# Batch 0's raw f32 products with 128 columns of phi instead of 64, and the expert probabilities loaded after the first key and value blocks

## The chip, the cores and the metric

The kernel runs on one core of one Trainium2 chip. The metric is the device time of one execution in microseconds (us). The engines are named as in the profile: PE (TensorE matmul) with PEld (its weight loads), DVE (VectorE), ACT (ScalarE), POOL (GpSimd) and SP (SyncE, which issues the DMAs).

## The reference

Eight batches, eight heads, 576 rows, head size 64, 32 memory slots. Attention goes over a compressed memory, and its output feeds a mixture of four experts.

```python
a = softmax(phi)                              # (8, 8, 576, 32), over the 32 slots
k_m = einsum('bhsm,bhsd->bhmd', a, k)         # 32 compressed keys for each head
v_m = einsum('bhsm,bhsd->bhmd', a, v)
attn = softmax(q @ k_m.T / sqrt(64))
x = (attn @ v_m), heads side by side          # (4608, 512)
p = domain_probs / (domain_probs.sum(-1) + 1e-9)
out = sum over e of p[:, e] * (relu(x @ w1[e]) @ w2[e])      # 512 -> 1024 -> 512
```

## The kernel before

**The long part.** The batches are worked in four pairs. For each pair and each expert the kernel folds the compressed values into w1 (tile `vw`), so that a step is: `first_mm` (L518 to L520, softmaxed scores `AT` times `vw`), a relu on ACT and a residual on DVE, and `second` (L562 to L564, times `w2`). Each f32 operand is split into a high and a low part, three products in place of one. These steps fill nearly all of the time. The end of a step group scales by `p` from tile `pt`, which `probabilities()` has normalized.

**The start.** Until the first step can run, batch 0 must be prepared. This is the place of the change:

- `load_phi(0)` and then the loads of `pt` and of six tiles (`stage`: the raw keys and values `kv` of four head pairs, their last 64 rows `kvt`, and a block of q, `qm`) are issued on SP's queue, which runs in order.
- `keep_warm(10)` issues ten products of the identity with itself on PE (`warm`, L1747) while the loads are under way.
- phi's softmax is done in the transposed layout and turned by PE (`tpa`, `tpb`) into the tile `af`.
- `direct_mm(hp, w, ...)` multiplies, in plain f32, the raw keys (w = 0) or values (w = 1) of head pair hp as the stationary operand by 64 columns of `af` (32 slots for each of the two heads) as the moving one: four products of 128 rows (L278) and one with the tail of 64 rows (L279), summed in PSUM tile `xd`. In the profile each such f32 product is two matmul records, each with its weight load of 128 columns. There are eight calls, four head pairs by two. I call them groups 1 to 8 in the order in which they run.
- Of the product of two heads' values with two heads' slots only the diagonal blocks are wanted. `direct_pick` copies them from `xd` to `kvT`.
- `scores_mm` (L408, `sc`) multiplies q by the compressed keys, `direct_vw` (L292, `pv`) the compressed values by raw w1. On DVE `scores_max`, `scores_sub`, `soft_sum` and `soft_mul` (L418, L426, L437, L444) with an exponential on ACT make the softmax, and PE turns it (`tp`, L457) into `AT`.

**What sets the order.** `start_plan` lists these pieces as tasks with a cost, dependencies and due times, simulates the engines with them, and emits the code in the order of the simulated starts. Loads that are under way at the start have assumed landing times in `LANDED`; a task whose `lands` is set isn't started in the plan before that time. Each engine runs its own instructions in the order in which they were emitted.

A load whose buffer is still in use waits on SP's queue until that buffer is released (`free_key`), and the loads behind it wait too. The raw key and value tiles are released by the second product that reads them, in groups 5 to 8.

Of the kernel before, what the change touches and what calls it, by code (L numbers as in the profile page):

```python
# [9 lines left out]
F32 = mybir.dt.float32  # L10
# [6 lines left out]
B, H, S, D, M = 8, 8, 576, 64, 32  # L17
N, DM, E, F = 4608, 512, 4, 1024
P = 128
# [32 lines left out]
START_SIDE = 1400  # L52
START_LOOK = 150
GHOST = 4
LANDED = (7900, 8600, 9900, 11200, 12500, 13800, 16500, 17800, 19100, 15200)
START_AT = 27500
LEAD = 2000
HOLD = 2500
# [10 lines left out]
def body(ctx: ExitStack, tc: tile.TileContext, qm, qt, qh, kv, kvt, phi, phn, prob, w1, w2, res):  # L69
    nc = tc.nc  # L70
    pool = lambda name, **k: ctx.enter_context(tc.tile_pool(name=name, bufs=1, **k))
    const, wp, work, att = pool("const"), pool("wp"), pool("work"), pool("att")
    psum = pool("psum", space=PSUM)
# [3 lines left out]
    kvT = [const.tile([P, 2, NP, 2 * M], F32, name=f"kvT{i}") for i in range(2)]  # L77
    for t in kvT:
        nc.gpsimd.memset(t, 0.0)
    pt = const.tile([P, N // P, E], F32, name="pt")  # L80
# [31 lines left out]
    def stage_ahead(upto):  # L112
        while count[0] < min(upto, len(order)):
            i, src = count[0], source(order[count[0]])
            tag, bufs = ring(i)
            t = work.tile([P, 1024], F32, name="stage", tag=tag, bufs=bufs)
            n = 1
            for d in src.shape[1:]:
                n *= d
            names = "abcd"[:len(src.shape) - 1]  # L120
            t = t[:src.shape[0], :n].rearrange(
                f"p ({' '.join(names)}) -> p {' '.join(names)}", **dict(zip(names, src.shape[1:]))
            )
            nc.sync.dma_start(t, src)
            staged[i] = t
            count[0] += 1
# [13 lines left out]
    def take_key(key):  # L140
        assert order[count[1]] == key and count[1] in staged, (key, count)
        raws[key] = staged.pop(count[1])
        count[1] += 1

    def free_key(key):
        del raws[key]
        released.add(numbers[key])
        stage_released()
# [21 lines left out]
    def w1_hi(raw, fh, hp):  # L170
        t = w1t[fh, hp] = new_w1()
        nc.scalar.copy(t[:, 0, :], raw[:, hp % 2, :])
# [5 lines left out]
    def w2_hi(j):  # L178
        t = w2t[0, 0, j] = wp.tile([P, 2, DM], F32R, name="w2", tag="w2", bufs=NJ)
        nc.scalar.copy(t[:, 0, :], raws["w2", 0, j // 2][:, j % 2, :])  # L180
# [6 lines left out]
    st = {}  # L187

    def load_phi(b):
        ph = att.tile([P, 2, 640], F32, name="ph", tag="ph")  # L190
        for g in range(2):
            nc.sync.dma_start(ph[:, g, :S], phi[b, g])
        st["ph", b] = ph

    def phi_max(b, g):
        nm = att.tile([P, 1], F32, name="nm", tag="nm", bufs=2)
        nc.vector.reduce_max(nm, st["ph", b][:, g, :S], AX.X)
        nc.vector.tensor_scalar_mul(nm, nm, -1.0)
        st["nm", b, g] = nm

    def phi_exp(b, g):
        ph = st["ph", b][:, g, :S]
        zs = att.tile([P, 1], F32, name="zs", tag="zs", bufs=2)
        nc.scalar.activation(ph, ph, AF.Exp, bias=st["nm", b, g], accum_out=zs)
        st["zs", b, g] = zs

    def phi_norm(b, g, tail=True):
        ph, zs = st["ph", b][:, g], st["zs", b, g]
        nc.vector.tensor_scalar_add(zs, zs, 1e-9)
        nc.vector.reciprocal(zs, zs)  # L210
        nc.vector.tensor_scalar_mul(ph[:, :S], ph[:, :S], zs)
        if tail:
            nc.vector.tensor_copy(ph[:, S:], ph[:, 512:S])
# [58 lines left out]
    def direct_mm(hp, w, raw, tail):  # L272

        if hp % 2 == 0:
            st["xd", w, hp // 2] = psum.tile([P, 2, 2 * M], F32, name="xd", tag="pm", bufs=4)
        x, af = st["xd", w, hp // 2][:, hp % 2, :], st["af"]
        for c in range(4):
            nc.tensor.matmul(x, raw[:, c, w, :], af[:, hp, c], start=c == 0, stop=False)  # L278
        nc.tensor.matmul(x, tail[:64, hp, w * P:w * P + P], af[:64, hp, 4], start=False, stop=True)  # L279
        if (hp, w) == (NP - 1, 1):  # L280
            free_key(("kvt", 0))

# [14 lines left out]
    def direct_vw_hi(ps, fh, g):  # L297
        vw[0, 0, fh, g] = att.tile([P, 2, 512], F32R, name="vw", tag="vw0", bufs=4)
        nc.scalar.copy(vw[0, 0, fh, g][:, 0, :], ps)
# [3 lines left out]
        nc.vector.tensor_sub(t[:, 1, :], ps, t[:, 0, :].bitcast(F32))  # L303

    def direct_pick(g, w, i):
        kvd, x = kvT[0][:, w, 2 * g:2 * g + 2], st["xd", w, g]
        r, m = slice(64 * i, 64 * i + 64), slice(M * i, M * i + M)
        (nc.vector.tensor_copy if i and w == 0 else nc.scalar.copy)(kvd[r, :, m], x[r, :, m])

# [10 lines left out]
    def kv_hi(b, hp, raw, c2):  # L320
        t = att.tile([P, 4 * TH], F32R, name="kvs", tag="kvs", bufs=KVS)
        t = t[:, :1024].rearrange("p (s i d) -> p s i d", s=2, i=2)
        nc.scalar.copy(t[:, 0], raw[:, 2 * c2:2 * c2 + 2].rearrange("p c w d -> p c (w d)"))
        st["kvs", b, hp, c2] = t
# [272 lines left out]
    def task(eng, cost, fn, *deps, **k):  # L597
        t = Task(eng, cost, fn, deps, **k)
        tasks.append(t)
        return t  # L600

    TA = lambda n, fn, *deps, **k: task("ACT", 90 + 0.93 * n, fn, *deps, **k)
    TD = lambda n, fn, *deps, **k: task("DVE", 90 + 1.05 * n, fn, *deps, **k)
# [3 lines left out]
    def start_plan(loads):  # L607
# [38 lines left out]
                take_key(key)  # L646

        task("SP", 1600, more, tasks[-1])
        TD(400, lambda: probabilities(), sb=True)
        xd, ka, kb, vf_ = {}, {}, {}, {}  # L650
        for hp in range(NP):
            for w in range(2):
                g = hp // 2
                key = ("kv", 0, hp)
                m = TP_(
                    1120, lambda hp=hp, w=w: direct_mm(hp, w, raws["kv", 0, hp], raws["kvt", 0]),
                    turned[g], turned[2], xd.get((hp - 1, w)) if hp % 2 else None,
                )
# [10 lines left out]
        for w in range(2):  # L669
            for g in range(2):  # L670
                ts = [xd[2 * g + i, w] for i in range(2)]
                a = TA(128, lambda g=g, w=w: direct_pick(g, w, 0), *ts)
                b = (TD if w == 0 else TA)(128, lambda g=g, w=w: direct_pick(g, w, 1), *ts, a)
                b.drop.append(heads_[g, w])
                picks[g, w] = b
                if w:
                    vf_[g] = TA(128, lambda g=g: direct_v(g), a, b)
        w0 = []
        for g in range(2):
# [4 lines left out]
            a = TA(512, lambda g=g, box=box: direct_vw_hi(box["p"], 0, g), t)  # L684
# [5 lines left out]
        for g in range(2):  # L690
            a = TD(576, lambda g=g: phi_max(1, g), alloc=["nm"])
            a.lands = "phi"
            b = TA(700, lambda g=g: phi_exp(1, g), a, alloc=["zs"])
# [3 lines left out]
        for j in range(NJ):  # L697
            key = ("w2", 0, j // 2)
            a = TA(512, lambda j=j: w2_hi(j))
# [18 lines left out]
        for g in range(2):  # L718
# [4 lines left out]
            a = TA(512, lambda g=g, box=box: direct_vw_hi(box["p"], 1, g), t)  # L723
# [58 lines left out]
        for hp in range(NP):  # L782
            key = ("kv", 1, hp)
            mms = []
            for c2 in range(2):
                a = TA(512, lambda hp=hp, c2=c2: kv_hi(1, hp, raws["kv", 1, hp], c2), kvl, alloc=["kvs"])
# [14 lines left out]
                if hp % 2 == 0 and c2 == 0:  # L801
                    mms[-1].alloc.append("pm")
                    x = mms[-1]
# [33 lines left out]
        for i in range(2 * NP):  # L837
            fh, hp = divmod(i, NP)
            key = ("w1", 0, fh, hp // 2, 1)
            a = TA(512, lambda fh=fh, hp=hp, key=key: w1_hi(raws[key], fh, hp))  # L840
# [76 lines left out]
        def landed(i):  # L917
            if i < len(early):
                return LANDED[i]
            if i in land:  # L920
# [9 lines left out]
        while left:  # L930
            best = None
            for eng in free:
                cand = None
                for t in left:
# [11 lines left out]
                    if t.lands is not None:  # L946
                        at0 = max(at0, LANDED[t.lands] if t.lands != "phi" else LANDED[-1])
                    ok = True
                    for r in t.alloc:
                        if len(ring[r]) >= RINGS[r]:  # L950
                            x = ring[r][-RINGS[r]]
# [747 lines left out]
    def run_task(t):  # L1699
        if t.take is not None:  # L1700
            take_key(t.take)
        t.fn()
        if t.free is not None:
            free_key(t.free)
# [31 lines left out]
    def probabilities():  # L1736
        z = att.tile([P, 1, N // P], F32, name="pz", tag="pz")
        nc.vector.reduce_sum(z[:, 0, :], pt, AX.X)
        nc.vector.tensor_scalar_add(z, z, 1e-9)
        nc.vector.reciprocal(z[:, 0, :], z[:, 0, :])  # L1740
        nc.vector.tensor_mul(pt, pt, z[:, 0, :].unsqueeze(2).broadcast_to([P, N // P, E]))

    def keep_warm(n):

        t = psum.tile([P, P], F32, name="warm", tag="pm", bufs=4)
        for _ in range(n):
            nc.tensor.matmul(t, ident, ident, start=True, stop=True)  # L1747

    load_phi(0)
    nc.sync.dma_start(pt, prob)  # L1750
    with tc.manual_schedule():
        stage_ahead(6)
        for key in early[:6]:
            take_key(key)
        keep_warm(10)
        engine.update(DVE=nc.vector, POOL=nc.gpsimd, ACT=nc.scalar)
        for g in range(2):
            phi_max(0, g)
        for g in range(2):
            phi_exp(0, g)  # L1760
        for g in range(2):
            phi_norm(0, g, False)
        write_vt(1)
        for t in first_tasks:
            run_task(t)
# [43 lines left out]
```

## Time and profile before

| | us |
|---|---|
| median of 3 runs | 1382.24 |
| the three runs | 1381.07 to 1382.52 |
| the profiled execution's own time | 1380.01 |
| its span, first to last instruction | 1378.2 |
| PE busy in the span | 1368.0 (99%) |
| DVE busy | 826.4 (60%) |
| ACT busy | 733.4 (53%) |
| mean granted PE clock | 0.993 of full speed |

All durations below are from that one profiled execution. It ran 2.2 us shorter than the median. Between its time and its span lie 1.8 us. In rows of the timeline the first number is the start in us from the span's start, the second how long the merged instructions took, and "xN" is the number of records. A matmul's duration includes its way through the array, and successive ones overlap; what PE takes per record is the distance from start to start, called the pitch here.

### The profile page before, as it was taken

Reading aid. Unit: us, or ns where it says so; the run is one execution under the profiler, and the core shown is the slowest. Engines: PE = TensorE matmul, PEld = TensorE weight load, DVE = VectorE, ACT = ScalarE, POOL = GpSimd, SP = SyncE. Lnnn points to the kernel's source line nnn. Section 1 sums busy time; section 2 is a strip of 40 time slices with the busy share of each in tenths; the row PEclk is TensorE's granted clock in tenths of the full one; section 3 lists DMA queues with packets and bytes.
Section 4 is the critical chain, followed back from the end, with each engine's and each line's share of the span. In section 5 each row is a group of like instructions: output and inputs, shape, how many; then the busy total and the mean of one; then the engine's idle time right before and its main releaser. Section 6 shows DMA issues by size and latency. Waiting matters only on the chain.

```text
span 1378.2 us, 21742 instructions
## 1 busy us (share of the span) xinstructions
PE 1368.0 (99%) x7444; PEld 1193.0 (87%) x7444; DVE 826.4 (60%) x1834; ACT 733.4 (53%) x1723; POOL 16.3 (1%) x20
## 2 busy tenths in 40 slices
PE   8999999999999999999999999999999999999998
PEld 7888888888888888888888888888888888888887
DVE  3776667577576655666567565665666644444532
ACT  3555555446656556565554656565665645455321
POOL 1210000000000000000000000000000000000000
PEclk7999999999999999999999999999999999999999
DMA  7486354253666566463664657456465545546101
GB/s 243 144 262 208 116 162 147 76 188 123 180 193 180 143 181 187 157 180 89 182 181 125 209 163 194 134 164 167 137 189 152 169 108 167 139 123 166 33 32 39
DMA packets 102910, 211.25 MB, mean 153 GB/s; under 512 B 18256, under 2 KB 18640, under 8 KB 102800
## 3 DMA queue, kind: packets, MB, share of 16 engines
q1 hardware_dynamic: 102800, 209.86, 51.1%
q8 instruction: 59, 0.97, 0.3%
q14 instruction: 51, 0.42, 0.1%
HBM read 133.24 MB, written 26.21 MB: 116 GB/s over the span
## 4 chain that ended last, share of the span: by engine, by line
PE 96%; DMA 2%; DVE 1%; ACT 1%; issue 0%; SPq 0%; ACTq 0%; DVEq 0%
PE p L564 19%; PE p L562 19%; PE p L563 19%; PE p L518 10%; PE p L520 10%; PE p L519 10%; PE pv L1174 3%; PE x L339 2%; PE sT L1490 1%; PE xd L278 1%; PE pv L292 1%; DMA stage<-in_kv 1%; DMA stage<-w 1%; PE sc L408 0%; PE pv L481 0%; PE pv L483 0%
## 5 line engine op out<-in xcount | busy, mean ns | idle before, releaser
L540 DVE SCALAR_TENSOR_TENSOR h<-p,h 128x256 fp32r<-128x256 f32 x512 | 215.5, 421 | 322.5 <-ACT h L534 190.8
L564 PE MATMUL p<-w,h 128*128 128x512 f32 x1024 | 403.7, 394 | 0.0
L562 PE MATMUL p<-w,h 128*128 128x512 f32 x1024 | 401.6, 392 | 0.0
L563 PE MATMUL p<-w,h 128*128 128x512 f32 x1024 | 400.6, 391 | 0.0
L534 ACT ACTIVATE h<-p 128x256 fp32r<-128x256 f32 x512 | 196.3, 383 | 323.9 <-PE p L520 305.4
L518 PE MATMUL p<-AT,vw 128*128 128x256 f32 (+1 forms) x1024 | 305.1, 298 | 1.4 <-ACT E L1182 1.3
L520 PE MATMUL p<-AT,vw 128*128 128x256 f32 (+1 forms) x1024 | 302.8, 296 | 0.3 <-DVE vw L499 0.3
L519 PE MATMUL p<-AT,vw 128*128 128x256 f32 (+1 forms) x1024 | 301.5, 294 | 0.2 <-DVE AT L471 0.2
L564 PEld LDWEIGHTS p<-w,h 128*128 128x128 f32 x1024 | 192.1, 188 | 43.2
L518 PEld LDWEIGHTS p<-AT,vw 128*128 128x128 f32 x1024 | 192.8, 188 | 23.3 <-ACT E L1182 2.8
L563 PEld LDWEIGHTS p<-w,h 128*128 128x128 f32 x1024 | 192.2, 188 | 22.4
L562 PEld LDWEIGHTS p<-w,h 128*128 128x128 f32 x1024 | 192.7, 188 | 21.8
L519 PEld LDWEIGHTS p<-AT,vw 128*128 128x128 f32 x1024 | 192.9, 188 | 19.9 <-DVE AT L471 0.6
L520 PEld LDWEIGHTS p<-AT,vw 128*128 128x128 f32 x1024 | 193.0, 188 | 0.6 <-DVE vw L499 0.6
L1182 ACT COPY E<-pv 128x512 f32<-128x512 f32 x192 | 111.3, 592 | 76.2 <-PE pv L1174 49.9
L540 DVE SCALAR_TENSOR_TENSOR hm<-p,hm 128x64 fp32r<-128x64 f32 x256 | 56.0, 219 | 157.2 <-ACT h L534 154.2
L534 ACT ACTIVATE hm<-p 128x64 fp32r<-128x64 f32 x256 | 56.6, 221 | 113.0 <-PE p L520 112.8
L1170 ACT CAST w<-stage 128x1024 fp32r<-128x1024 f32 x96 | 100.7, 1049 | 4.7 <-DMA stage<-w 4.7
L1256 DVE TENSOR_TENSOR w<-stage,w 128x512 fp32r<-128x512 f32 x120 | 79.4, 682 | 0.0
L1252 ACT CAST w<-stage 128x512 fp32r<-128x512 f32 x120 | 73.3, 616 | 6.4 <-DMA stage<-in_w 6.2
L1236 DVE TENSOR_TENSOR vw<-rows,vw 128x512 fp32r<-128x512 f32 x96 | 64.7, 686 | 10.7 <-ACT vw L1232 10.0
L584 DVE SCALAR_TENSOR_TENSOR acc<-p,pt,acc 128x512 f32<-128x512 f32 x96 | 67.3, 742 | 2.7 <-PE p L564 2.6
(150 smaller groups left out, 1307.9 us busy)
## 6 DMA issues: line engine op xcount, KB each, us to landing
stage<-w SPq DMA_DIRECT2D x96, 512.0 KB, 4.2
rows<-E SPq DMA_DIRECT2D x768, 64.0 KB, 2.8
stage<-in_w SPq DMA_DIRECT2D x84, 512.0 KB, 4.1
stage<-in_kv SPq DMA_DIRECT2D x32, 512.0 KB, 4.5
w<-w SPq DMA_DIRECT2D x64, 256.0 KB, 4.8
out<-acc SPq DMA_DIRECT2D x32, 256.0 KB, 4.1
stage<-in_qh SPq DMA_DIRECT2D x24, 288.0 KB, 3.5
ph<-in_phi SPq DMA_DIRECT2D x16, 288.0 KB, 4.0
```

Of the source, the lines that this page charges most:

```text
L518: nc.tensor.matmul(ps, w[:, 0, f], at_t[:, g, 0, c], start=g == 0, stop=False)
L519: nc.tensor.matmul(ps, w[:, 0, f], at_t[:, g, 1, c], start=False, stop=False)
L520: nc.tensor.matmul(ps, w[:, 1, f], at_t[:, g, 0, c], start=False, stop=g == 1)
L534: nc.scalar.activation(t[:, 0, to], ps[:, at_], AF.Relu)
L540: nc.vector.scalar_tensor_tensor(t[:, 1, to], ps[:, at_], 0.0, t[:, 0, to].bitcast(F32), ALU.max, ALU.subtract)
L562: nc.tensor.matmul(po[t], x[:, 0, :], w[:, 0, :], start=j == 0, stop=False)
L563: nc.tensor.matmul(po[t], x[:, 0, :], w[:, 1, :], start=False, stop=False)
L564: nc.tensor.matmul(po[t], x[:, 1, :], w[:, 0, :], start=False, stop=j == NJ - 1)
L1170: nc.scalar.copy(w, raws[key])
L1182: nc.scalar.copy(box["E"][:, i, :], box[i])
L1252: nc.scalar.copy(t[:, 0, :], raws[key][:, i, :])
L1256: nc.vector.tensor_sub(t[:, 1, :], raws[key][:, i, :], t[:, 0, :].bitcast(F32))
```

## The change

The moving operand of `direct_mm` becomes the 2 x 64 columns of both head pairs of a half (hp = 0, 1 or hp = 2, 3) instead of the 64 of its own pair. The PSUM tile doubles, and `direct_pick` reads every third block of 64 columns, which are the ones that were computed before. Further, `pt` is loaded after the six first tiles instead of ahead of them, `probabilities()` is planned no earlier than phi's landing time, and the landing times assumed by the plan are 100 to 300 ns later.

```diff
-LANDED = (7900, 8600, 9900, 11200, 12500, 13800, 16500, 17800, 19100, 15200)
+LANDED = (8000, 8700, 10000, 11300, 12600, 13900, 16800, 18100, 19400, 15500)
...
-            st["xd", w, hp // 2] = psum.tile([P, 2, 2 * M], F32, name="xd", tag="pm", bufs=4)
-        x, af = st["xd", w, hp // 2][:, hp % 2, :], st["af"]
+            st["xd", w, hp // 2] = psum.tile([P, 2, 2, 2 * M], F32, name="xd", tag="pm", bufs=4)
+
+        x, af = st["xd", w, hp // 2][:, hp % 2], st["af"][:, hp // 2 * 2:hp // 2 * 2 + 2]
         for c in range(4):
-            nc.tensor.matmul(x, raw[:, c, w, :], af[:, hp, c], start=c == 0, stop=False)
-        nc.tensor.matmul(x, tail[:64, hp, w * P:w * P + P], af[:64, hp, 4], start=False, stop=True)
+            nc.tensor.matmul(x, raw[:, c, w, :], af[:, :, c], start=c == 0, stop=False)
+        nc.tensor.matmul(x, tail[:64, hp, w * P:w * P + P], af[:64, :, 4], start=False, stop=True)
...
-        kvd, x = kvT[0][:, w, 2 * g:2 * g + 2], st["xd", w, g]
+        kvd, x = kvT[0][:, w, 2 * g:2 * g + 2], st["xd", w, g].rearrange("p a b m -> p (a b) m")[:, ::3]
...
-        TD(400, lambda: probabilities(), sb=True)
+        TD(400, lambda: probabilities(), sb=True).lands = "phi"
...
     load_phi(0)
-    nc.sync.dma_start(pt, prob)
     with tc.manual_schedule():
         stage_ahead(6)
         for key in early[:6]:
             take_key(key)
+        nc.sync.dma_start(pt, prob)
```

PE, groups 3 to 5 of `xd` with the first scores behind group 4; `af` is phi's softmax, `stage` a raw tile, and the last numbers are the output's shape. Before:

```order
L278 MATMUL xd_207<-af_164,stage_126 128x64 x4
L279 MATMUL xd_207<-af_164,stage_122 128x64
L278 MATMUL xd_207<-af_164,stage_128 128x64 x4
L279 MATMUL xd_207<-af_164,stage_122 128x64
L408 MATMUL sc_220<-kvT0_75,stage_130 128x64 x4
L278 MATMUL xd_227<-af_164,stage_120 128x64 x4
L279 MATMUL xd_227<-af_164,stage_122 128x64
L408 MATMUL sc_220<-kvT0_75,stage_130 128x64 x4
```

The same place on PE in the changed kernel (its lines lie one further down):

```order
L279 MATMUL xd_202<-af_164,stage_125 128x128 x4
L280 MATMUL xd_202<-af_164,stage_121 128x128
L279 MATMUL xd_202<-af_164,stage_127 128x128 x4
L280 MATMUL xd_202<-af_164,stage_121 128x128
L409 MATMUL sc_215<-kvT0_75,stage_129 128x64 x4
L279 MATMUL xd_222<-af_164,stage_119 128x128 x4
L280 MATMUL xd_222<-af_164,stage_121 128x128
L409 MATMUL sc_215<-kvT0_75,stage_129 128x64 x4
```

Nothing moved on PE: the same products in the same order, with 128 columns in `xd`. This holds for PE's whole program, and ACT's and POOL's orders are the same as well.

DVE, from the last piece before the picks (`vt`) to the first half of the softmax; `pz` and `pt` belong to `probabilities()`, `nm` to phi of batch 1. Before:

```order
L395 TENSOR_TENSOR vt_159<-kvT1_76,vt_159 128x2x64 x2
L1738 TENSOR_REDUCE pz_172<-pt_79 128x36
L1739 TENSOR_SCALAR pz_172<-pz_172 128x36
L1740 RECIPROCAL pz_172<-pz_172 128x36
L1741 TENSOR_TENSOR pt_79<-pt_79,pz_172 128x144
L308 COPY kvT0_75<-xd_196 64x2x32
```

DVE in the changed kernel, where these four instructions now stand, between the subtraction of the maximum and the sum of the exponentials:

```order
L419 TENSOR_REDUCE mx_247<-sc_215 128x16
L427 TENSOR_TENSOR at_251<-sc_215,mx_247 128x512
L1739 TENSOR_REDUCE pz_260<-pt_79 128x36
L1740 TENSOR_SCALAR pz_260<-pz_260 128x36
L1741 RECIPROCAL pz_260<-pz_260 128x36
L1742 TENSOR_TENSOR pt_79<-pt_79,pz_260 128x144
L438 TENSOR_REDUCE z_267<-at_251 128x16
```

Only these four moved on DVE. On SP's queue only the load of `pt` moved, behind the six first loads.

## The prediction

> **What bounds the kernel now.** I read the page first: PE is busy 99% of the span, and its granted clock is full but for the start.
>
> ```profile
> PE 1368.0 (99%) x7444; PEld 1193.0 (87%) x7444; DVE 826.4 (60%) x1834; ACT 733.4 (53%) x1723; POOL 16.3 (1%) x20
> PEclk7999999999999999999999999999999999999999
> ```
>
> So the time is the work that PE has to stream, and whatever makes the steps start earlier ends the kernel earlier by as much, as long as nothing else comes too late. The one digit below 9 is the first fortieth (34 us). I cut that stretch into windows where the clock changes; the columns are window, length, busy time of PE, PEld, DVE, ACT and POOL with counts, granted clock, DMA share, GB/s.
>
> ```profile
> 6.77:10.18 3.41, 2.77 (x20) 2.19 (x20) 2.34 (x10) 1.75 (x5) 0.00 (x0) 1.00 1.01 279
> 10.18:13.60 3.42, 2.70 (x21) 2.36 (x20) 0.23 (x1) 0.20 (x1) 0.00 (x0) 1.00 1.02 403
> 13.60:17.00 3.40, 3.40 (x15) 3.05 (x14) 0.00 (x0) 0.20 (x1) 0.00 (x0) 0.50 1.04 406
> ...
> 27.20:30.65 3.45, 3.45 (x13) 3.10 (x14) 2.37 (x2) 0.80 (x3) 1.33 (x1) 0.50 0.45 182
> 30.65:34.06 3.41, 3.41 (x5) 1.34 (x5) 0.00 (x0) 0.82 (x5) 0.00 (x0) 0.50 0.74 269
> 34.06:37.50 3.44, 3.44 (x13) 1.70 (x12) 1.75 (x3) 1.58 (x3) 0.00 (x0) 1.00 0.94 302
> ```
>
> From 13.6 to 34.06 us PE runs at half clock, without a gap in its busy time. That is 20.5 us, six windows of 3.41, and it ends after the first one that held nothing but `pv`. What PE did there is in the timeline:
>
> ```profile
> 1.78 4.64 PE L1747 MATMUL warm<-ident 128*128 128x128 f32 x20 [1.78 <-POOL ident masks.py:199]
> ...
> 8.92 1.08 PE L278 MATMUL xd<-af,stage 128*128 128x64 f32 x8 [0.29 <-DMA stage<-in_kv]
> ...
> 11.13 1.10 PE L278 MATMUL xd<-af,stage 128*128 128x64 f32 x8 [0.72 <-DMA stage<-in_kv]
> 12.17 0.43 PE L279 MATMUL xd<-af,stage 64*128 64x64 f32 x2
> 12.53 1.10 PE L278 MATMUL xd<-af,stage 128*128 128x64 f32 x8
> ...
> 14.18 1.97 PE L278 MATMUL xd<-af,stage 128*128 128x64 f32 x8
> 16.08 0.69 PE L279 MATMUL xd<-af,stage 64*128 64x64 f32 x2
> 16.69 1.97 PE L408 MATMUL sc<-kvT,stage 128*128 128x64 f32 x8
> 18.45 1.91 PE L278 MATMUL xd<-af,stage 128*128 128x64 f32 x8
> ...
> 27.65 1.97 PE L278 MATMUL xd<-af,stage 128*128 128x64 f32 x8
> ...
> 30.16 5.62 PE L292 MATMUL pv<-stage,af 128*128 128x512 f32 x8
> 35.62 0.60 PE L457 MATMUL tp<-ident,at 128*128 128x128 f32 x4
> 36.06 1.88 PE L292 MATMUL pv<-stage,af 128*128 128x512 f32 x4
> 37.38 0.68 PE L518 MATMUL p<-AT,vw 128*128 128x256 f32 x1
> ```
>
> ```profile
> L278 PE MATMUL xd<-af,stage x24: 275/275/323, 8.9 to 13.4; 128*128 128x64 f32 x24
> L278 PE MATMUL xd<-af,stage x40: 421/421/473, 14.2 to 29.2; 128*128 128x64 f32 x40
> L1747 PE MATMUL warm<-ident x20: 421/421/582, 1.8 to 6.0; 128*128 128x128 f32 x20
> ```
>
> The last fence has minimum, median and maximum duration of one record in ns (L278 early, L278 late, warm). 421 ns marks the half clock. `warm` has it too, so the 1.00 shown ahead of 6.8 us is no measurement; the record of the clock begins with its first switch.
>
> **The cost of the added columns.** Pitches follow from a merged row: length, less the last record's duration, over the records less one. `warm`, 128 columns at half clock: (4.64 - 0.42)/19 = 0.222 us. `xd`, 64 columns at half clock: (1.97 - 0.42)/7 = 0.221. The same, so there the weight load paces both and the second 64 columns pass behind it. At full clock `xd` takes (1.10 - 0.275)/7 = 0.118. No row shows 128 columns of f32 at full clock; `pv` with 512 takes (1.88 - 0.59)/3 = 0.43, so 128 stream in about 0.107, still under 0.118. Inside a run I take nothing. Where L278 and L279 change over, the pitch is longer: 12.17 - 11.13 is 1.04 for eight records and group 2 takes 12.53 - 11.13 = 1.40 for ten, 0.22 over 10 x 0.118. There the weight load may wait for the stream ahead, which is now 54 ns longer. Bounds: nothing, and 54 ns at each of four slow distances, 0.21 a group. I take the two changes of line, 0.1: a group is 1.50 at full clock (1.40 to 1.61), against 2.51 at half (14.18 to 16.69).
>
> **What the columns do to the clock.** At half clock a record of 64 columns streams for about 0.107 of its 0.221 us, 48%; one of 128 for 96%. Five windows (13.6 to 30.65) at about that share left the clock at half, though PE counted as busy in all of them. One window of `pv` restored it, and 4.6 us of `warm` did so ahead of 6.8 us. So I take streaming, not busy time, as what the clock follows, and `warm` shows that 128 columns of f32 are enough. It fell after two windows (6.77 to 13.6) of 41 records, ten that turn phi and the rest `xd`; by 54 ns each that is 2.2 of 6.83 us, 32%. With 107 ns for each `xd` the same stretch would have 3.8 us, 56%. The threshold for rising lies above about 48%; of the one for falling the rows say only that it is above 32%. I take it that the clock mostly stays full; if it falls once, the next window of `xd` raises it.
>
> **The sum, with the clock full.** Group 2 waits for its raw tile. `pt`'s load no longer stands ahead:
>
> ```profile
> 1.64 0.43 SPq L1750 DMA_DIRECT2D pt<-in_prob  x1
> 5.23 0.45 SPq L124 DMA_DIRECT2D stage<-in_qm  x1
> 20.40 0.33 SPq L124 DMA_DIRECT2D stage<-in_w  x1
> 20.00:21.00 1.00, 1.00 (x5) 0.77 (x4) 0.00 (x0) 0.00 (x0) 0.00 (x0) 0.50 0.00 0
> ```
>
> At most 0.43 us earlier, at least nothing; the DMA engines are full there (share 1.02), so most but not all: group 2 starts at 10.8. Seven groups at 1.50 are 10.5, two `sc` at half of 18.45 - 16.69 are 1.8. Group 8 ends at 10.8 + 10.5 + 1.8 = 23.1 instead of 30.16: 7.1 us. The eight `pv` take 8 x 0.43 = 3.4 instead of 35.62 - 30.16 = 5.5: 2.0 us. From `tp` on the clock was full before, too. Sum 9.1 us (8.0 with the long group and no earlier load, 9.9 with the short one).
>
> **Who must keep up.** The loads issued by 10 us had landed by 20.0 us (DMA share 0 from 20 to 21), before `pv` starts at 23.1. The next load of w1, issued at 20.40 when group 5 had read its tile, now goes out near 17.4. DVE and ACT have this to do ahead of `tp`:
>
> ```profile
> 8.02 0.30 DVE L1738 TENSOR_REDUCE pz<-pt 128x36 f32<-128x144 f32 x1
> 8.98 0.31 DVE L1741 TENSOR_TENSOR pt<-pt,pz 128x144 f32<-128x144 f32 x1
> 22.92 0.69 DVE L418 TENSOR_REDUCE mx<-sc 128x16 f32<-128x512 f32 x1 [3.83 <-PE sc L408]
> 23.64 0.69 DVE L426 TENSOR_TENSOR at<-sc,mx 128x512 f32<-128x512 f32 x1
> 26.01 0.69 DVE L437 TENSOR_REDUCE z<-at 128x16 f32<-128x512 f32 x1 [1.68 <-ACT at L431]
> 27.23 0.69 DVE L444 TENSOR_TENSOR at<-at,z 128x512 f32<-128x512 f32 x1
> ```
>
> The second `sc` would end at 10.8 + 4 x 1.5 + 1.8 = 18.6. Maximum and subtraction end at 20.1. `probabilities()` takes 8.02 to 9.29, 1.3 us, in the gap where DVE waits for the exponential (1.68 us before, nearer 0.9 now, since group 6 no longer holds ACT as long): about 0.4 us comes through, to 21.4. Sum to product took 27.92 - 26.01 = 1.9: done at 23.3. `tp` comes at 26.5. So 3.2 us of room cover it, and also a late `pt`: its load, issued after 5.2 us behind 2 MB, has landed by 20 as all others have. If the cover went, only what exceeds 3.2 us would count. What is late next is the pair `vw` and `AT` behind the last `pv` and `tp`, in the same distance as before.
>
> Against the profiled time: 1380.01 - 9.1 = **1370.9**. That execution was 2.2 us below the median of 1382.24 and 1.1 below the lowest run, so against the median I forecast 0.8% less. I don't shift the sum by it, since the other runs may only have met the clock's windows at a worse point.
>
> **Rivals.**
>
> *The clock still falls, for one or two windows.* Each costs half of 3.41 us: 1372.6 or 1374.3. For it: the fall came after windows with waits for loads in them, which stay (group 1 to group 2), and `sc` still streams at 48%. Against it: 56% instead of 32%.
>
> *The clock goes by busy time, and something else holds it down.* Then the groups pass at half clock with 0.2 us more each, five of them: 1381. Against it: busy 3.40 of 3.40 us at 0.50. [...]
>
> *Slower: the columns don't hide.* Each of 70 records in groups 2 to 8 then takes 0.107 us more at half clock: 7.5 us, 1387.5. It needs the clock to stay down too, since at full clock 70 x 0.054 = 3.8 us leave a gain (9.8 - 3.8 = 6.0). It decides from 40 ns a record on. Against it stands `warm` with 128 columns at 0.222. [...]
>
> *A new wait takes about half.* DVE or a load arrives 4 to 5 us after PE: 1375.4. For it: the softmax and the w2 splits now have 9 us less ahead of the steps; against it the 3.2 us of room.
>
> **How the numbers follow.** Clock held 0.50 (1370.9), one or two windows lost 0.34 (1372.6 to 1374.3), new wait 0.06, no reaction 0.06, columns add 0.04. A measurement tells about 0.2%, 2.8 us, from no change; the first three are faster: 0.90, no reaction is the same: 0.06, slower 0.04. The range goes from 1369.0 (the sum at its bound, 1370.1, and 1 us for the spread of the runs, 1.45 us) to 1375.0 (two lost windows, 1374.3, and the same for long groups), which leaves out 0.16 and some.
>
> **What would show it.** Right: granted clock 1.00 between 17 and 34 us, L278 (now L279) with 128 columns near 275 ns a record, group 8 done near 23, the first L518 (now L519) near 28.3, `pz` near 20 without a wait for `pt`. Wrong: 421 ns records up to 25 us or later; a wait of PE for DVE or a load ahead of `tp`; or an L518 that is 9 us earlier and an end that isn't, which would be a limit further on that no row here shows.

## The result: 0.7% faster, with the clock full through the start

| | us |
|---|---|
| before, median of 4 runs | 1381.65 (1378.11 to 1382.52) |
| changed, median of 4 runs | 1372.05 (1370.84 to 1372.79) |
| ratio, with its 95% interval | 0.9934 (0.9915 to 0.9954) |
| changed, the profiled execution: time, span | 1370.84, 1369.1 |

The change was measured a second time, with 6 runs: 1372.55 (1371.95 to 1373.81), ratio 0.9941 (0.9929 to 0.9954). The rows of the page that answer to those shown of before, PE's busy time and the granted clock in 40 slices:

```profile
PE 1358.4 (99%) x7444; PEld 1184.7 (87%) x7444; DVE 826.7 (60%) x1834; ACT 734.1 (54%) x1723; POOL 16.4 (1%) x20
PEclk9999999999999999999999999999999999999999
```

PE has 9.6 us less busy time with the same 7444 matmul records: they are the same records, and fewer of them ran at half clock. The first digit of the clock went from 7 to 9. The same windows as before (length, busy time of PE, PEld, DVE, ACT, POOL, then granted clock, DMA share, GB/s):

```profile
10.18:13.60 3.42, 3.29 (x22) 2.81 (x23) 0.23 (x1) 0.20 (x1) 0.00 (x0) 1.00 1.02 394
13.60:17.00 3.40, 3.40 (x27) 3.04 (x27) 1.77 (x4) 0.80 (x2) 0.00 (x0) 1.00 1.05 411
17.00:20.40 3.40, 3.40 (x27) 3.04 (x27) 2.12 (x7) 1.79 (x6) 0.00 (x0) 1.00 0.89 267
27.20:30.65 3.45, 3.45 (x18) 2.25 (x18) 2.52 (x7) 1.59 (x4) 0.00 (x0) 1.00 0.97 331
```

Between 13.6 and 17.0 us PE worked on 27 records instead of 15 (granted clock 1.00 instead of 0.50), and its busy time is 3.40 us in both: busy time doesn't show the clock. PE's timeline:

```profile
8.28 1.06 PE L279 MATMUL xd<-af,stage 128*128 128x128 f32 x8
...
10.31 1.16 PE L279 MATMUL xd<-af,stage 128*128 128x128 f32 x8 [0.49 <-DMA stage<-in_kv]
11.40 0.49 PE L280 MATMUL xd<-af,stage 64*128 64x128 f32 x2
11.81 1.16 PE L279 MATMUL xd<-af,stage 128*128 128x128 f32 x8
...
22.21 0.48 PE L280 MATMUL xd<-af,stage 64*128 64x128 f32 x2
22.62 3.70 PE L293 MATMUL pv<-stage,af 128*128 128x512 f32 x8
26.16 0.60 PE L458 MATMUL tp<-ident,at 128*128 128x128 f32 x4
26.60 1.88 PE L293 MATMUL pv<-stage,af 128*128 128x512 f32 x4
27.91 0.68 PE L519 MATMUL p<-AT,vw 128*128 128x256 f32 x1
```

A group takes 11.81 - 10.31 = 1.50 us at full clock. The `pv` begin at 22.62 instead of 30.16 and the first step at 27.91 instead of 37.38 us, 9.5 us earlier.

### The profile page after: what moved, and what is told of

The parts are those of the page before. It is cut to its first block, busy times and chain, and to the rows that moved or that the text cites. A ratio compares the mean times of both kernels' runs of the same rounds, so it can differ in the third digit from the quotient of the medians.

```text
span 1369.1 us, 21741 instructions
## 1 busy us (share of the span) xinstructions
PE 1358.4 (99%) x7444; PEld 1184.7 (87%) x7444; DVE 826.7 (60%) x1834; ACT 734.1 (54%) x1723; POOL 16.4 (1%) x20
## 4 chain that ended last, share of the span: by engine, by line
PE 97%; DMA 1%; DVE 1%; ACT 1%; issue 0%; SPq 0%; DVEq 0%
PE p L565 19%; PE p L563 19%; PE p L564 19%; PE p L519 10%; PE p L521 10%; PE p L520 10%; PE pv L1175 3%; PE x L340 2%; PE sT L1491 1%; DMA stage<-in_kv 1%; PE xd L279 1%; PE pv L293 1%; PE pv L482 0%; PE pv L484 0%; PE pv L483 0%; DMA stage<-in_w 0%
```

## The experiments

**Which half of the change did it?** First the columns alone, with `pt` loaded first again, and then the move of `pt` alone.

```diff
 columns_only, against the changed kernel
+    nc.sync.dma_start(pt, prob)                       # straight behind load_phi(0) again
-        nc.sync.dma_start(pt, prob)                   # no longer behind the six tiles
-        TD(400, lambda: probabilities(), sb=True).lands = "phi"
+        TD(400, lambda: probabilities(), sb=True)     # and LANDED as before
 pt_only, against the changed kernel
-        x, af = st["xd", w, hp // 2][:, hp % 2], st["af"][:, hp // 2 * 2:hp // 2 * 2 + 2]
+        x, af = st["xd", w, hp // 2][:, hp % 2, hp % 2], st["af"]
-            nc.tensor.matmul(x, raw[:, c, w, :], af[:, :, c], ...)
+            nc.tensor.matmul(x, raw[:, c, w, :], af[:, hp, c], ...)
```

> The 128 columns alone; the load of pt, probabilities() and the assumed landing times stand as before. If the streamed columns hold the clock: no window at half clock after 7 us, group 2 begins about where it did before (10.7 to 11.1 instead of 10.3 us), groups of 1.50 us, first step at about 28.5, and 1371.3 to 1373, at most 1 us above the changed kernel. If the move of pt made the gain: fall at 13.6 as before and 1379 to 1382.

> Only the move of pt and of probabilities(); the products have 64 columns as before. If the columns hold the clock: it falls to half at one of the window ends between 10 and 17 us and stays there until the first pv have filled a window (32 to 36 us); group 2 begins 0.4 to 0.8 us sooner; 1379 to 1382, no change within 0.2%. If the move of pt made the gain: about 1371 and full clock.

Columns alone: 1374.45 us (1371.73 to 1375.87), ratio 0.9948 (0.9932 to 0.9964). `pt` alone: 1380.2 us (1377.75 to 1382.76), ratio 0.999 (0.9981 to 1.0). So the columns carry most, and the move of `pt` alone is worth 0.1% (0.2% at most). The columns alone came out 1.5 us above the 1373 that I had as the most; their interval overlaps that of the changed kernel (0.9915 to 0.9954), so four runs don't tell the two apart. In the profiled execution the clock fell once. Windows of columns_only, and two rows of its PE timeline:

```profile
6.60:10.04 3.44, 2.66 (x18) 1.99 (x18) 2.50 (x10) 1.91 (x6) 0.00 (x0) 1.00 1.01 256
10.04:13.46 3.42, 2.38 (x15) 1.98 (x16) 0.07 (x1) 0.21 (x1) 0.00 (x0) 0.99 1.02 406
13.46:16.87 3.41, 3.41 (x15) 2.96 (x14) 0.16 (x1) 0.00 (x0) 0.00 (x0) 0.50 1.05 408
16.87:20.30 3.43, 3.43 (x27) 2.95 (x25) 1.95 (x5) 1.32 (x4) 0.00 (x0) 1.00 0.51 197
```

```profile
10.59 0.46 PE L280 MATMUL xd<-af,stage 64*128 64x128 f32 x2 [0.67 <-DMA stage<-in_kvt]
11.54 1.16 PE L279 MATMUL xd<-af,stage 128*128 128x128 f32 x8 [0.50 <-DMA stage<-in_kv]
```

PE waited for the raw tiles twice (0.67 and 0.50 us); after the two windows to 13.46, with these waits in them, the clock fell for one window, and the next one, filled with 128-column records at half clock, raised it (0.50 from 13.46 to 16.87 us, 1.00 behind). That is the first rival of the prediction, in the kernel without the second part of the change. The six windows at half clock of the kernel before shrink to one.

That the waits, and the fall, come from `pt`'s load being ahead is not shown. The changed kernel, profiled a second time (after_again, below), has `pt` behind the tiles, waited almost as long at the same places, and kept its clock:

```profile
5.70:9.11 3.41, 2.47 (x20) 2.02 (x20) 1.99 (x8) 2.64 (x9) 0.00 (x0) 1.00 1.03 240
9.11:12.52 3.41, 2.43 (x17) 1.84 (x15) 0.00 (x0) 0.16 (x1) 0.00 (x0) 1.00 1.02 402
```

```profile
10.03 0.46 PE L280 MATMUL xd<-af,stage 64*128 64x128 f32 x2 [0.50 <-DMA stage<-in_kvt]
10.96 1.16 PE L279 MATMUL xd<-af,stage 128*128 128x128 f32 x8 [0.47 <-DMA stage<-in_kv]
```

In pt_only, on the other side, groups 1 to 4 followed each other without any wait, and the clock still fell, near 15.1 us, and came back only after about 6 us of `pv`, near 32 us (0.52 from 28.90 to 32.30 us). Windows of pt_only:

```profile
8.39:11.80 3.41, 3.41 (x29) 3.14 (x27) 0.23 (x1) 1.03 (x3) 0.00 (x0) 1.00 1.02 401
11.80:15.20 3.40, 3.40 (x28) 3.13 (x27) 0.96 (x2) 0.21 (x1) 0.00 (x0) 0.98 1.05 406
15.20:18.60 3.40, 3.40 (x16) 3.16 (x16) 0.99 (x4) 1.72 (x4) 0.00 (x0) 0.50 0.86 292
32.30:35.70 3.40, 3.40 (x18) 2.15 (x17) 1.31 (x3) 1.66 (x3) 0.00 (x0) 1.00 0.94 370
```

PE was busy for all of 6.81 us (8.39 to 15.20) and the clock fell at their end (the 0.98 comes from their last 0.1 us). No gap explains it; what is small is the share that 64 columns stream: by the 0.43 us of a `pv` record with 512 columns some 0.054 us each, 0.54 of the 1.40 us of a group (an estimate).

**Does useless streaming hold the clock?** 64 columns again, and ahead of groups 2 to 8 four products of the identity with itself, which the group then overwrites.

```diff
+        for _ in range(4 if (hp, w) != (0, 0) else 0):
+            nc.tensor.matmul(x, ident, ident, start=True, stop=True)     # 128 columns
+        x = x[:, hp % 2]                                                 # then 64 columns
```

> As the changed kernel, but the products have 64 columns, and ahead of each of groups 2 to 8 four products of the identity with itself (128 columns, 8 records) are put in, whose results are overwritten: useless work. If what the clock follows is streaming: share about 58% in groups 2 to 8, clock full, a group 1.40 us and 0.94 us for the four; 7 x 0.94 less 7 x 0.1 and less the 0.5 us of waiting that the first four fill, so 5.4 us above the changed kernel, about 1376 to 1378, still 4 us below the kernel before. If the clock isn't reached by streaming and only shorter PE work helps: half clock to past 40 us, some 7 x 1.9 us more than before, 1390 or more.

1376.29 us (1375.69 to 1376.6), ratio 0.9962 (0.9948 to 0.9976), as expected. A window of fill4 where the kernel before had half clock, and a filled group in its PE timeline:

```profile
17.40:20.80 3.40, 3.40 (x30) 3.27 (x29) 1.66 (x4) 1.72 (x4) 0.00 (x0) 1.00 0.17 27
```

```profile
12.15 1.16 PE L279 MATMUL xd<-ident 128*128 128x128 f32 x8
13.15 1.00 PE L282 MATMUL xd<-af,stage 128*128 128x64 f32 x8
14.08 0.43 PE L283 MATMUL xd<-af,stage 64*128 64x64 f32 x2
14.44 1.16 PE L279 MATMUL xd<-ident 128*128 128x128 f32 x8
```

28 f32 products more, done for nothing, made the kernel 5 us faster than before. But for these products it is the kernel of pt_only, which took 1380.2 us. So it is not the shape of these products, nor the loads, that gained: it is the clock, and added streaming alone kept it full (1.00 from 7.2 to 24.2 us).

**Where do the columns stop being free?** 256, 96 and 80 columns instead of 128.

```diff
 cols256
-        x, af = st["xd", w, hp // 2][:, hp % 2], st["af"][:, hp // 2 * 2:hp // 2 * 2 + 2]
+        x, af = st["xd", w, hp // 2][:, hp % 2], st["af"]       # tile xd: all four head pairs
...                                                          # direct_pick reads the wanted blocks
 cols96, cols80 (af laid out with the pairs' columns side by side; n = 96 or 80)
+        lo = 0 if hp % 2 == 0 else P - n
+        x, at_ = x[:, lo:lo + n], slice(hp // 2 * P + lo, hp // 2 * P + lo + n)
+            nc.tensor.matmul(x, raw[:, c, w, :], af[:, c, at_], ...)
```

> As the changed kernel, but all four head pairs' 256 columns pass each time. The clock should stay full as with 128. The columns no longer hide behind the weight load: from pv (512 columns, 0.43 us) 256 columns stream for 0.215 us against a pitch of 0.118, so a group takes 10 x 0.215 plus some 0.3, about 2.4 us instead of 1.5: 7 x 0.9 = 6.3 us more than the changed kernel, 1377 to 1379, and the first step near 34.5. If columns were hidden in any number, or only the order of the loads counted: 1371 to 1372.

> As the changed kernel, but 96 columns pass, the pair's own 64 and 32 of its neighbour. By the pitch of pv 96 columns stream for 0.080 us at full clock, so a group of about 1.45 us streams for 55%, with the scores some 53% between 8.4 and 15.2 us. The clock fell so far at 40 to 44% and held at 55% and more. If the threshold is one half, it holds or loses one window: 1371 to 1374, first step between 27.5 and 30. If it takes clearly more than half, it falls, and rises again after one or two windows (62% at half clock): 1373 to 1375.

> As before with 80 columns: 0.067 us each at full clock, 47% of a group of 1.42 us, and 0.133 us at half clock, 52% of a group of 2.55 us. If one half is the threshold both ways: the clock falls near 15 us and rises again after one to three windows, 1372 to 1378. If rising takes clearly more (60% or over): half clock up to the first pv, as with 64 columns, 1378 to 1382. If the clock goes by whether 64 columns are exceeded at all: no fall, 1371 to 1372.

256 columns: 1382.15 us (1380.26 to 1382.77), ratio 1.0003 (0.9993 to 1.0013). The clock was full (a mean of 1.0 in the profiled execution), and nothing was left of the gain. PE's timeline of cols256:

```profile
8.96 1.99 PE L279 MATMUL xd<-af,stage 128*128 128x256 f32 x8 [0.46 <-ACT af L260]
...
11.51 1.99 PE L279 MATMUL xd<-af,stage 128*128 128x256 f32 x8
...
28.59 1.99 PE L279 MATMUL xd<-af,stage 128*128 128x256 f32 x8
...
36.44 0.68 PE L519 MATMUL p<-AT,vw 128*128 128x256 f32 x1
```

A group takes 14.06 - 11.51 = 2.55 us, where I had expected 2.4, and group 1, which used to end in a wait for a tile, now pushes group 2 from 10.31 to 11.51: 1.2 + 7 x 1.05 = 8.5 us, the whole distance of the first steps (36.44 - 27.91). The forecast of 1377 to 1379 missed by leaving group 1 out (1.2 us) and by 0.15 us a group (1.05). Behind the first step the profiled execution took 2.2 us longer than that of the changed kernel, too; the wait that the end of this section deals with makes 0.4 us of it (1.7 instead of 1.3), and the rest is not explained.

96 columns: 1372.55 us over ten runs (1370.67 to 1384.4), ratio 0.9943 (0.9923 to 0.9962), first step at 27.3. 80 columns: 1371.61 us (1370.13 to 1373.38), ratio 0.9922 (0.9905 to 0.9938), first step at 26.75, since a group takes 1.42 us. Both are no different in time from 128. In 80 the start of the profiled execution was at full clock throughout (1.00 from 4 to 40 us), against both branches of my expectation that had the clock fall. By the pitches, 80 columns stream for about 47% of 8.4 to 15.2 us (the windows of pt_only). The falls came after two windows at 32% (before), 40% (pt_only) and some 44% (columns_only). All these shares are estimates: the records of a stretch, each at its columns' part of the 0.43 us that a `pv` record with 512 takes. They would put the threshold for falling between 44% and 47%, a little below the half that I had in mind, but the runs do not settle it. The count takes 54 ns for each of the ten records that turn phi, and these have 128 columns. PE's timeline of the kernel before:

```profile
6.94 0.66 PE L255 MATMUL tpa<-ident,ph 128*128 128x128 f32 x4 [0.52 <-DVE zs L209]
7.76 0.66 PE L255 MATMUL tpa<-ident,ph 128*128 128x128 f32 x4 [0.16 <-DVE ph L211]
8.25 0.38 PE L265 MATMUL tpb<-ident,ph 128*64 128x128 f32 x2
```

At 107 ns for each of them the kernel before comes to an estimated 40% and columns_only to some 50%, above the 47% that kept the clock. And the changed kernel profiled again stands at about 44%, too, from 5.70 to 12.52 us by the first count (an estimate), and kept it. The third branch of my expectation, that the clock goes by whether 64 columns are exceeded at all, is what 80 columns alone would show; against it stands the fall of columns_only.

One of ten runs with 96 columns took 1384.4 us at a mean granted clock of 0.991, which is what the kernel before shows. So 96 columns did not always hold the clock; none of the ten runs of the changed kernel is like that, and its group costs 0.05 us more.

**Joined tails.** The tail product first in every second group, so that two tails follow each other.

```diff
...
+        ops = last_ + main if hp % 2 else main + last_      # the 64-row tail first or last
...
```

> The changed kernel with the 64-row product first in every second group, so that the tails of two groups follow each other (three pairs of groups have no scores in between). Of the 0.1 us by which each change between 128 and 64 rows lengthens a pitch, six fall away: first step at about 27.3 instead of 27.9, and 0.5 us less in the end, 1370.3 to 1372.3, within what this measurement tells from the changed kernel. If the longer pitches belong to the tail's own load and not to the change of rows: no difference in the first step.

PE's timeline of tails:

```profile
21.65 3.60 PE L295 MATMUL pv<-stage,af 128*128 128x512 f32 x8
...
26.84 0.68 PE L521 MATMUL p<-AT,vw 128*128 128x256 f32 x1
```

The first step came at 26.84, 1.07 us earlier instead of 0.6. The waits for tiles differ a little between these two executions; in two executions of the last experiment below (PHI_ODD 38), neither of which has such a wait, the first step comes at 27.34 and with joined tails at 26.24, 1.10 us apart. So the longer pitches do belong to the change between 128 and 64 rows: six changes fewer saved about 1.1 us, 0.18 each, and the saving is larger than I had put it. The time, 1371.26 us (1370.66 to 1374.38), ratio 0.9927 (0.9913 to 0.9942), can't be told from the changed kernel's.

**How much room had DVE?** Four reductions of 0.75 us more in `probabilities()`.

```diff
+        for _ in range(4):
...
+            nc.vector.reduce_max(idle, st["ph", 1][:, 0, :S], AX.X)
```

> The changed kernel with four more reductions of 128x576 (0.75 us each, 3.0 us in all) in probabilities(), whose result nobody reads. By the prediction's 3.2 us of room ahead of tp nothing comes through: first step at 27.9. By the changed kernel's trace DVE's own queue has less: w2's residual ends at 24.46 and the two residuals of vw wait 0.80 and 1.03 us for ACT, so 3.0 less 1.8, 1.2 us, comes through: tp in time, AT's residual about 1.2 us later, and PE waits that long ahead of L520's products, span 1370 to 1372.

DVE's timeline of dve3, with POOL's one row, and the same two of the changed kernel:

```profile
20.78 3.11 DVE L1745 TENSOR_REDUCE idle<-ph 128x1 f32<-128x576 f32 x4
25.62 0.69 DVE L184 TENSOR_TENSOR w<-stage,w 128x512 fp32r<-128x512 f32 x1
26.22 1.36 DVE L304 TENSOR_TENSOR vw<-pv,vw 128x512 fp32r<-128x512 f32 x2
22.11 1.27 POOL L184 TENSOR_TENSOR w<-stage,w 128x512 fp32r<-128x512 f32 x1 [19.24 <-ACT w L180]
```

```profile
22.70 1.76 DVE L184 TENSOR_TENSOR w<-stage,w 128x512 fp32r<-128x512 f32 x1
22.44 1.47 POOL L184 TENSOR_TENSOR w<-stage,w 128x512 fp32r<-128x512 f32 x1 [19.57 <-ACT w L180]
```

First step at 27.82 and one time of 1371.82 us: nothing came through, but neither reason was right. The residual of w2 (L184) shrank from 1.76 to 0.69 us, and that gave back the 1.1 us that DVE's queue lacked. In dve3 POOL's half of the same work was over (at 23.38) when DVE began its own; in the changed kernel DVE began while POOL was at work and ended 0.55 us after it (24.46 and 23.91).

**Where do the runs differ?** The runs of the changed kernel spread over 1.9 us in each of two measurements, 3.0 us in all, and behind the first step the profiled executions so far part mainly at one place of the steps, near 508 us in the changed kernel, where PE waits 1.3 us for DVE. There the queue of SP (SPq in the rows) waits for a load of w with the row moves (`rows`) behind it. I moved the loads of phi that precede these moves two steps ahead, in the changed kernel, with the joined tails, and in the kernel before.

```diff
-PHI_EVEN, PHI_ODD = 0, 40
+PHI_EVEN, PHI_ODD = 0, 38
```

> The changed kernel once more, unaltered, for the spread of its runs and for the place near 508 us where PE waited 1.3 us for DVE. If the start is right as explained, every run has full clock up to there and lies between 1370 and 1374; what differs is that one wait (0 to 2.5 us), and the median is 1371.5 to 1372.8, not the 1370.9 that was worked out against an execution of the kernel before that had no such wait. If the clock is only held by luck at the start, some runs show a granted clock of 0.997 or less and 1374 or more.

> The changed kernel with PHI_ODD 38 instead of 40: the loads of the odd batches' phi are planned two steps earlier, and the order of the later steps changes with them. If those loads (2 x 288 KB ahead of the row moves on SP's queue) make the wait near 508 us: the wait is gone, the runs lie within 1 us of each other, median 1370.3 to 1371. If the wait comes from the moves and the loads of w themselves: no difference, median 1371.5 to 1372.8.

> The joined tails (first step at 26.84 instead of 27.91 us) together with PHI_ODD 38. If both help: 1369.3 to 1370.3, the best so far. If only the tails do: 1370.5 to 1371.7. If the start's gain is given back at the wait near 508 us: 1371.5 to 1372.8, like the changed kernel.

> The kernel before (64 columns, pt first) with PHI_ODD 38 alone: the change measured again without the wait near 508 us. If the change is worth what its first 38 us show, 9.5 us less whatever the clock's windows add or take, this kernel lies 9 to 11 us above the changed kernel with PHI_ODD 38 (1369.19), 1378 to 1380.5, and what spread is left (two or three us) goes with the number of windows at half clock. If the changed kernel gained part of its lead from the later order, the distance is under 8 us.

| | median (lowest to highest), us | ratio to before |
|---|---|---|
| changed, again | 1372.55 (1371.95 to 1373.81) | 0.9941 (0.9929 to 0.9954) |
| changed, PHI_ODD 38 | 1369.19 (1368.98 to 1369.21) | 0.9916 (0.9901 to 0.9931) |
| changed, joined tails, PHI_ODD 38 | 1367.88 (1367.8 to 1368.56) | 0.9908 (0.9893 to 0.9923) |
| before, PHI_ODD 38 | 1378.75 (1376.57 to 1381.08) | 0.998 (0.9969 to 0.9991) |

Waits between 470 and 525 us (engine, line, releaser: total, times, longest), in the changed kernel:

```profile
PE p L519 <- DVE h L541: 1.3, 1, 1.3
SPq L1193 <- DMA stage<-w: 2.3, 2, 1.7
```

and in the changed kernel with PHI_ODD 38, where PE waits for nothing in this stretch:

```profile
SPq L1193 <- DMA stage<-in_qh: 0.7, 1, 0.7
```

The wait is gone, and the spread of the runs with it (0.23 us). The median fell by 3.4 us, more than I had expected and more than the wait of 1.3 to 1.6 us. The profiled executions of after_again (1372.68 us) and phi38 (1369.19) lie near these medians. Their first steps come at 28.56 and 27.34: 1.2 of the 3.5 us arise at the start, where after_again has the two waits for tiles shown above and phi38 none. The orders of the two kernels are the same for the first 149 us, so this part isn't the edit's doing. The other 2.3 us come later. Since the edit also changes the order of other steps, it stays open what it gained besides the wait, and whether it was these loads that made the wait. The profiled execution of the kernel before had no such wait: neither row is there in this stretch.

With the wait out of the way the change is worth 1378.75 - 1369.19 = 9.6 us by the medians, about what its first 38 us say. The two were measured on different chips; by their ratios to the kernel before beside each (0.998 and 0.9916) it is 0.6%, 8.8 us. The two profiled executions lie closer, 1376.57 (the lowest of twelve) and 1369.19: their first steps come at 35.16 and 27.34, 7.8 us apart. By my estimate the kernel before was at half clock for one window less at the start there: of the 2.2 us by which its first step came sooner than in its first profile (35.16 and 37.38), 0.5 are shorter waits for tiles (0.5 instead of 1.0), and the other 1.7 are half of 3.41. What spread is left in the kernel before with PHI_ODD 38, 4.5 us, goes with its mean clock, 0.993 in the shortest run and 0.991 in the longest. The kernel with joined tails and PHI_ODD 38 beats both, at 1367.88, below the 1369.3 to 1370.3 that I had expected.

Behind the long wait of cols80 came a second loss. In its profiled execution PE stood for 1.90 us of 510 to 512.3 us, and then the clock fell in the middle of the steps:

```profile
510.00:512.00 2.00, 0.40 (x2) 0.00 (x0) 0.40 (x2) 2.00 (x5) 0.00 (x0) 1.00 0.50 117
512.00:514.00 2.00, 1.70 (x9) 1.59 (x10) 1.72 (x4) 1.42 (x6) 0.00 (x0) 0.87 0.79 235
514.00:516.00 2.00, 2.00 (x7) 1.63 (x6) 1.40 (x4) 0.79 (x3) 0.00 (x0) 0.50 1.02 361
516.00:518.00 2.00, 2.00 (x10) 1.83 (x9) 0.81 (x3) 0.72 (x3) 0.00 (x0) 0.78 0.88 166
```

The wait alone does not decide it: in columns_only PE waited 2.19 us at this place, and its mean clock of 0.999 holds the one window at the start (half of 3.41 us is 0.0012 of the span) and no second one. In tails, with 1.95 us, the mean is 0.999 too, though the start was at 1.00 from 4 to 40 us; whether it fell behind the wait is not shown.

## Why the prediction was right, point by point

- *The added columns cost 0.1 us a group.* Right: records of 128 columns took 275 ns in the median as those of 64 had at full clock, and a group 1.50 us, the value taken between 1.40 and 1.61. 256 columns showed the other side, 2.55.
- *The clock follows streaming, not busy time.* Right in the main. fill4 kept the clock with useless work (1.00 from 7.2 to 24.2 us), and pt_only lost it without a gap: PE was busy from 8.39 us on, and at half clock from 15.20 to 18.60. How much streaming is enough is open. The prediction's 32% is too low by its own count: the ten records that turn phi have 128 columns (rows of `tpa` and `tpb` above) and were taken as 64, and with 128 it is about 40% (both estimates). They are also rows of 128 f32 columns at full clock, of which the prediction said that there were none.
- *The clock held.* Right for the changed kernel, whose ten runs have a granted clock of 0.998 to 1.0. The one at 0.998 (1373.81 us) was probably at half clock for a window or more somewhere: one of 3.41 us takes 0.0012 off the mean (an estimate from the span of 1372.0 us), and the execution of cols80 with that mean had one near 513 us. The 56% that I gave as the reason does not make it safe: with waits for loads of 1.3 us (0.17, 0.67 and 0.50) columns_only lost a window, and with 1.0 us (0.50 and 0.47) after_again did not. Part of it is luck, then, and whether the move of `pt` held the clock up is open.
- *Group 2 at 10.8 us.* It began at 10.31, since group 1, too, began at 8.28 instead of 8.92, and so outside the bound of 0.43. In after_again it began at 10.96: when the tiles land differs from execution to execution.
- *9.1 us in sum.* The first step came 9.5 us earlier, the span is 9.1 us shorter: behind the first step 0.4 us were lost, the wait of 1.3 us near 508 us among them. That the spans agree with the sum to a tenth is luck: in after_again the first step comes at 28.56, 8.8 us earlier, and the span of 1370.9 is 7.3 us shorter.
- *1370.9 us.* The median was 1372.05, inside the range and 1.2 us above. The step that was off is the base. I called the 2.2 us between the profiled execution and the median a matter of the clock's windows; that may hold for part of the spread of the kernel before. Another part is probably the wait near 508 us, which that execution happened not to have, and which both profiled executions of the changed kernel have; only one execution of the kernel before was profiled, so whether its other runs had the wait is not shown.
- *3.2 us of room on DVE.* It covered `probabilities()`, as said, but was counted for `tp` alone. DVE's own queue had 1.8 us, and only the shorter L184 made it larger.
- *The rivals.* The clock's fall for a window came true in columns_only, the cost of added columns in cols256. In the profiled executions of the changed kernel neither occurred, nor that the clock doesn't react, nor that a new wait takes half.

## What to carry to other kernels

Where a matmul's pitch doesn't follow its columns (at half clock it was 0.221 us with 64 and 0.222 with 128), more columns can cost almost nothing: here 64 more took 0.10 us a group of ten records at full clock. And in these kernels the granted clock was 1.00 in the groups in which PE streamed for an estimated 61% of the time (fill4: 8 x 0.107 and 10 x 0.054 of 2.29 us) and 71% (the changed kernel: 10 x 0.107 of 1.50). So look for stretches where PE is busy and the clock is 0.50: here the work itself was too thin (64 columns, by the same estimate 38%, 10 x 0.054 of 1.40 us). And one profiled execution is one sample: before its time is used as the base of a sum, compare it with the runs, and look for a wait that others have and it has not.

## What the runs showed of the hardware that I had not expected

- The clock fell to half with PE busy for 100% of the two windows before (pt_only, 64 columns, an estimated 40% streamed), and it rose after one window of 3.41 us with 128-column records at half clock (columns_only). Each stretch recorded at half clock at the start was a whole number of 3.41 us: 20.48 (before), about 17.1 (pt_only) and 3.41 us (columns_only).
- A wait of 1.90 us in the steps was followed by one window at half clock (cols80, near 513 us), while a wait of 2.19 us at the same place (columns_only, mean clock 0.999) was not.
- The same DVE instruction (128x512, L184) took 1.76 us when it began while POOL worked on its half of the split (before and the changed kernel), and 0.69 us when POOL had finished (dve3).
- A change between 128 and 64 rows of the stationary operand lengthened PE's pitch: joining three pairs of tails saved 1.07 us, and 1.10 us between two executions without waits for tiles.
